# A fused two-block transformer kernel on one core: the second x chunk in two loads, and another order on each engine

## The chip, the cores and the metric

The kernel runs on one core of one Trainium2 chip. The metric is the time of one execution in device microseconds (us). The kernel before has a median of 393.72 us over three executions (392.11, 393.72 and 393.86). One further execution was profiled: 391.6 us, of which 389.9 us are the span between the first and the last instruction that the profile holds.

Five engines of the core take part: TensorE (PE, matrix products; PEld is its weight load), VectorE (DVE), ScalarE (ACT), GpSimd (POOL) and SyncE (SP), which here only issues DMA transfers. Each engine works through its own list in order. An instruction that waits for a semaphore holds up everything behind it in its list.

## The reference

The input is x of shape (1, 2048, 448) in bf16. Two kinds of block alternate, each with a residual connection: A (attention), B (gated), A, B, with the same weights both times.

```python
def _A_ref(x, wqkv, wo):
    B, S, D = x.shape
    H = 16; Dh = D // H
    W, dil = 8, 2
    qkv = (lambda x, *d: x.transpose(*d))((x @ wqkv).reshape(B, S, 3, H, Dh), 2, 0, 3, 1, 4)
    q, k, v = qkv[0], qkv[1], qkv[2]
    scale = Dh ** -0.5
    pos = jnp.arange(S)
    off = jnp.arange(W) * dil
    idx = pos[:, None] - off[None, :]
...
    logits = jnp.einsum("bhsd,bhswd->bhsw", q, kg) * scale
    logits = jnp.where(mask[None, None, :, :], logits, -1e9)
    attn = _softmax(logits, axis=-1)
    o = jnp.einsum("bhsw,bhswd->bhsd", attn, vg)
    return (lambda x, *d: x.transpose(*d))(o, 0, 2, 1, 3).reshape(B, S, D) @ wo

def _B_ref(x, w_gate, w_up, w_down):
    g = jnp.einsum("bsd,df->bsf", x, w_gate)
    u = jnp.einsum("bsd,df->bsf", x, w_up)
    h = g * u
    return jnp.einsum("bsf,fd->bsd", h, w_down)

x = x + _A_ref(_layernorm(x, axis=-1), A_wqkv, A_wo)
x = x + _B_ref(_layernorm(x, axis=-1), B_w_gate, B_w_up, B_w_down)
x = x + _A_ref(_layernorm(x, axis=-1), A_wqkv, A_wo)
x = x + _B_ref(_layernorm(x, axis=-1), B_w_gate, B_w_up, B_w_down)
```

## The kernel before

The 2048 tokens are 16 blocks of 128, and four blocks are a chunk. The input and output hold even tokens first, then odd ones, so that the dilated window of the attention becomes eight neighbours. The four layers run interleaved by chunks: `SEQ` is "A00 A01 B10 A02 B11 A03 B12 A20 ...", where A01 is layer 0 (attention), chunk 1, and B10 is layer 1 (gated), chunk 0.

**Of one attention chunk.** DVE computes the statistics of each block (L763 and L765), ACT the inverse deviation (L766, L768), and DVE writes the normalised block `xn_sb` (L784). In chunks 0 and 1 of layer 0 (`PE_T`) PE transposes it with an identity matrix (L794), and ACT or DVE copies the result to `xnTa` (L801). Elsewhere SP issues a DMA that transposes (L787). PE then computes K and Q in four units per chunk (L834, weights `WQK`), which ACT or DVE copies out of PSUM to `qk` (L895), and V (L834, weights `WV`; copied by L948). Scores (L981) of a group of queries occupy four PSUM banks. ACT takes the exponential (L993), DVE multiplies by the mask (L1002), and PE applies the result to V (L1020). DVE and ACT normalise (L1044 to L1070). PE multiplies with the output weights `wo_g` (L854 or L1106), and DVE adds to `x_sb` (L1114).

**Of one gated chunk.** The normalised block is written twice over (`xn_sb` of 896 columns) and transposed by DMA to `xnTb` (L787). PE computes gate and up together (L1144, weights `WGU`), ACT copies the gate (L1150), DVE multiplies (L1153) into `hT`, and PE computes the down product (L854, weights `WD`). The first product of L1144 waits for all 14 loads of `WGU` and for the four transposes of its chunk.

**PSUM** has eight banks, and most work takes them in pairs. A pair comes free when its reader on ACT or DVE is through.

**At the start** PE multiplies zeros (L683) until data arrive. SP and ACT issue the loads: x chunk 0 in four loads of one block, the V weights in four, the K and Q weights into `hT` in four (DVE and ACT reorder them into `WQK`, L692), and then x chunks 1, 2 and 3 in one load each. The load of chunk 1 waits for one of the V weight loads. The loads of `WGU` and `WD` wait until x block 7, the last of chunk 1, has landed.

**What sets the order.** Each unit of work gets a number as it is created (`Sched.add`). The table `ORDER` holds, for each engine, these numbers in the order in which the engine is to work. The scheduler then only assigns PSUM banks and semaphores. When a load is added, all numbers behind it shift by one.

Of the kernel before, what the change touches and what calls it, by code (L numbers as in the profile page):

```python
# [15 lines left out]
NCH = S // 512  # L16
# [53 lines left out]
    ],  # L70
    "act": [
# [12 lines left out]
    ],  # L84
    "dve": [
# [476 lines left out]
def build(nc, A_x, A_wqkv, A_wo, B_w_gate, B_w_up, B_w_down, out):  # L562
# [85 lines left out]
    for q in range(1, 4):  # L648
        load_x(q, (0, 1, 1), "sp", 4100.0, -50 + q, deps=[("wv", 3)] if q == 1 else [], svc=(1350.0 if q == 1 else 2600.0, 1200.0))
# [660 lines left out]
```

## Time and profile before

| what | us |
|---|---|
| median of three executions | 393.72 |
| the profiled execution | 391.6 |
| its span | 389.9 |
| PE busy within it | 379.3 |
| DVE busy | 263.8 |
| ACT busy | 184.0 |

All times below are of the profiled execution, counted from the start of its span. A row of the timeline gives start, duration, engine, line, operation, output and input, the number of instructions merged, and in brackets how long the engine sat idle before it and what ended that. The duration of a merged row runs to the end of its last instruction, and neighbouring rows overlap by about 0.1 us where the engine is pipelined. SPq marks the time in which SP issues a transfer; the transfer itself lands later.

### The profile page before, as it was taken

The page shows a single profiled execution, that of the slowest core. Times are in us where ns is not written, and L with a number is a line of the kernel's source. Part 1 is how long each engine was busy: PE and PEld are TensorE (multiplying, and loading weights), DVE is VectorE, ACT ScalarE, POOL GpSimd, SP SyncE. Part 2 cuts the span into 40 slices and gives each one's busy share as a digit, 9 for nine tenths or more (in the row PEclk, how much of TensorE's full clock was granted, in tenths as well). Part 3 has the DMA queues.
Part 4 walks back from the last instruction along what each step waited for, and adds up shares of the span by engine and source line. Part 5 has one row for each costly group of instructions (what it writes and reads, how often), then busy time and mean ns, then how long its engine had stood idle before and what let it go on. Part 6 is the DMA issues. An engine that isn't in the chain of part 4 may idle for free.

```text
span 389.9 us, 12779 instructions
## 1 busy us (share of the span) xinstructions
PE 379.3 (97%) x5694; PEld 201.2 (52%) x5694; DVE 263.8 (68%) x579; ACT 184.0 (47%) x302; POOL 6.0 (2%) x24
## 2 busy tenths in 40 slices
PE   7898999999999999999999999999999999999997
PEld 5454555555444555545444674445545555555554
DVE  6898879789897657355894278955478857733513
ACT  4996874772561336475143465332577303332310
POOL 6000000000000000000000000000000000000000
PEclk9999999999999999999999999999999999999999
DMA  7959675013142262000072000180001050310002
GB/s 218 266 104 159 98 128 134 3 26 74 25 72 59 30 87 57 11 6 5 5 108 43 14 6 5 24 126 5 12 2 45 19 96 13 79 41 2 13 0 96
DMA packets 53630, 22.59 MB, mean 58 GB/s; under 512 B 44288, under 2 KB 52648, under 8 KB 53576
## 3 DMA queue, kind: packets, MB, share of 16 engines
q1 hardware_dynamic: 52856, 21.15, 28.4%
q8 instruction: 45, 0.74, 0.8%
q10 hardware_dynamic: 720, 0.63, 0.5%
q14 instruction: 9, 0.07, 0.1%
HBM read 8.53 MB, written 1.84 MB: 27 GB/s over the span
## 4 chain that ended last, share of the span: by engine, by line
PE 90%; ACT 3%; DVE 3%; DMA 2%; issue 1%; SPq 1%
PE ps L1144 43%; PE ps L854 23%; PE ps L834 15%; PE ps L1106 3%; PE ps L1020 2%; PE ps L981 2%; PE ps L1165 1%; PE ps L683 1%; DMA xnTb<-xn_sb 1%; DMA qk<-qk 1%; DVE x_sb L1114 1%; ACT g_sb L1150 1%; ACT qk L895 1%; ACT E_sb L993 1%; SPq L619 1%
## 5 line engine op out<-in xcount | busy, mean ns | idle before, releaser
L1144 PE MATMUL ps<-xnTb,WGU 64*128 64x512 bf16 x1568 | 176.5, 376 | 0.8 <-DMA xnTb<-xn_sb 0.3
L1144 PEld LDWEIGHTS ps<-xnTb,WGU 64*128 64x128 bf16 x1568 | 81.1, 94 | 87.0 <-issue 4.2
L1150 ACT ACTIVATE g_sb<-ps 128x512 bf16<-128x512 f32 x112 | 64.9, 594 | 106.4 <-PE ps L1144 95.6
L1153 DVE TENSOR_TENSOR hT<-g_sb,ps 128x512 bf16<-128x512 bf16 x112 | 74.4, 681 | 51.2 <-ACT g_sb L1150 49.7
L854 PE MATMUL ps<-WD,hT 64*128 64x448 bf16 x840 | 85.7, 349 | 0.1
L854 PEld LDWEIGHTS ps<-WD,hT 64*128 64x128 bf16 x840 | 44.1, 94 | 34.6 <-DVE hT L1153 0.8
L1114 DVE TENSOR_TENSOR x_sb<-x_sb,ps 128x448 bf16<-128x448 bf16 x62 | 36.0, 614 | 30.0 <-PE ps L854 24.6
L834 PE MATMUL ps<-xnTa,WQK 64*128 64x512 bf16 (+1 forms) x448 | 47.2, 357 | 1.3 <-ACT E_sb L993 1.2
L993 ACT ACTIVATE E_sb<-ps 128x1024 bf16<-128x1024 f32 (+1 forms) x36 | 33.7, 980 | 17.9 <-PE ps L981 17.7
L763 DVE BATCH_NORM_STATS2 st<-x_sb 128x6 f32<-128x448 bf16 x64 | 38.2, 613 | 3.0 <-DMA x_sb<-in_A_x_dram 2.9
L784 DVE TENSOR_SCALAR xn_sb<-x_sb,mv,rstd 128x512 bf16<-128x512 bf16 (+1 forms) x64 | 34.8, 567 | 1.7 <-DMA xnTb<-xn_sb 1.0
L834 PEld LDWEIGHTS ps<-xnTa,WQK 64*128 64x128 bf16 x448 | 22.1, 94 | 23.0 <-ACT E_sb L993 2.7
L834 PE MATMUL ps<-WV,xnTa 64*128 64x448 bf16 (+1 forms) x252 | 28.1, 340 | 1.2 <-ACT lnv L766 0.8
L895 ACT ACTIVATE qk<-ps 128x1024 bf16<-128x1024 f32 (+1 forms) x24 | 22.8, 967 | 12.5 <-PE ps L834 12.4
L1070 DVE TENSOR_TENSOR oT<-ps,R_sb 128x448 bf16<-128x448 f32 (+2 forms) x38 | 21.1, 598 | 9.5 <-ACT R_sb L1050 9.5
L1002 DVE TENSOR_TENSOR E_sb<-E_sb,MK 128x1024 bf16<-128x1024 bf16 (+2 forms) x40 | 23.5, 604 | 3.3 <-ACT E_sb L993 3.2
L948 ACT ACTIVATE v_sb<-ps 128x896 bf16<-128x896 f32 (+1 forms) x16 | 13.7, 868 | 20.5 <-PE ps L834 20.4
L1049 ACT ACTIVATE R_sb<-R_sb 128x960 f32<-128x960 f32 (+1 forms) x18 | 17.3, 959 | 7.7 <-DVE R_sb L1047 7.5
L766 ACT ACTIVATE lnv<-mv,eps_sb 128x2 f32<-128x2 f32 (+1 forms) x34 | 9.2, 292 | 20.2 <-DVE mv L765 19.9
L834 PEld LDWEIGHTS ps<-WV,xnTa 64*128 64x128 bf16 x252 | 12.7, 94 | 11.2 <-issue 1.2
L1050 ACT ACTIVATE R_sb<-R_sb 128x960 f32<-128x960 f32 (+1 forms) x18 | 17.3, 959 | 0.4
L981 PEld LDWEIGHTS ps<-qk 28*64 28x64 bf16 x1088 | 10.1, 103 | 9.8 <-issue 4.8
(47 smaller groups left out, 172.6 us busy)
## 6 DMA issues: line engine op xcount, KB each, us to landing
out_dram<-x_sb SPq DMA_DIRECT2D x15, 112.0 KB, 1.8
WGU<-in_B_w_gate_dram SPq DMA_DIRECT2D x7, 224.0 KB, 5.1
WGU<-in_B_w_up_dram SPq DMA_DIRECT2D x7, 224.0 KB, 4.3
WD<-in_B_w_down_dram SPq DMA_DIRECT2D x14, 112.0 KB, 2.6
x_sb<-in_A_x_dram SPq DMA_DIRECT2D x3, 448.0 KB, 5.9
hT<-in_A_wqkv_dram SPq DMA_DIRECT2D x3, 224.0 KB, 5.0
qk<-qk SPq DMA_DIRECT2D x24, 28.0 KB
xnTb<-xn_sb SPq DMA_TRANSPOSE x32, 3.2
```

The source lines that it names most:

```text
L763: sc.add("dve", one(lambda E, B=B: E.bn_stats(st6[:, B, :], x_sb[:, B, :]), ("bn", li, B)), 525.0, deps=[("x", li - 1, B)] + ([("xn", li - ...
L784: sc.add("dve", one(lambda E, B=B, dst=dst, src=src: E.tensor_scalar(dst, src, mv[:, B, 0:1], rstd[:, B:B + 1], ALU.subtract, ALU.mult), ( ...
L834: ins.append((lambda E, w=w, c=c, lo=lo, st=st, sp_=sp_: E.matmul(u["out"](w), u["lhs"](w, c, lo, lo + 64), u["rhs"](w, c, lo, lo + 64), s ...
L854: ins.append((lambda E, w=w, c=c, lo=lo, st=st, sp_=sp_: E.matmul(outs(w), lhs(w, c, lo), rhs(w, c, lo), start=st, stop=sp_), keys[w] if s ...
L895: return E.activation(dst, src, ACT.Copy) if hasattr(E, "activation") else E.tensor_copy(dst, src)
L993: return E.activation(E_sb[:, slot, 2 * hp:2 * hp + 2, 0:w], ps[:, b0:b0 + 2, 0:w], ACT.Exp, scale=SCALE)
L1002: return E.tensor_tensor(e, e, m, ALU.mult)
L1070: return E.tensor_tensor(dst, src, rec, ALU.mult)
L1114: sc.add("dve", one(lambda E: E.tensor_tensor(x_sb[:, B, :], x_sb[:, B, :], ps[:, bk[w], 0:D], ALU.add), ("x", li, B)), dve_est(D), deps=[ ...
L1144: ins.append((lambda E, u=u, k=k, w=w: E.matmul(u["out"](w), WGU[64 * w:64 * w + 64, k, 128 * u["fc"]:128 * u["fc"] + 128], X[64 * w:64 * ...
L1150: sc.add("act", one(lambda E, gs=gs, bk=bk: E.activation(g_sb[:, gs, 0:n], ps[:, bk[0], 0:n], ACT.Copy), ("G", li, jp, fc)), act_est(n), d ...
L1153: sc.add("dve", one(lambda E, gs=gs, bk=bk, fc=fc: E.tensor_tensor(hT[:, fc, hs, h0:h1], g_sb[:, gs, 0:n], ps[:, bk[1], 0:n], ALU.mult), ( ...
```

## The change

The load of x chunk 1 (blocks 4 to 7, 448 KB) becomes two loads, blocks 4 and 5, then 6 and 7, each with a semaphore of its own. The first waits for the same V weight load as the whole chunk did. The loads of chunks 2 and 3 keep their form.

```diff
@@ build @@
-    sem_names += [f"d_x{i}0" for i in range(NCH)] + [f"d_x0{p}" for p in range(1, 4)] + ...
+    sem_names += [f"d_x{i}0" for i in range(NCH)] + [f"d_x0{p}" for p in range(1, 4)] + ["d_x11"] + ...
...
-    for q in range(1, 4):
-        load_x(q, (0, 1, 1), "sp", 4100.0, -50 + q, deps=[("wv", 3)] if q == 1 else [], svc=(1350.0 if q == 1 else 2600.0, 1200.0))
+    for h in range(2):
+        load_x(1, (h, h + 1, 2), "sp", 3450.0, -49.1 + 0.05 * h, deps=[("wv", 3)] if h == 0 else [], svc=(700.0, 1200.0))
+    for q in range(2, 4):
+        load_x(q, (0, 1, 1), "sp", 4100.0, -50 + q, svc=(2600.0, 1200.0))
```

The figures 3450, 700 and so on are the scheduler's estimates. With a written `ORDER` they set nothing in the program. The table `ORDER` itself is replaced for all five engines; its first lines for PE show how:

```diff
     "pe": [
-        38, 39, 40, 41, 42, 43, 44, 45, 46, 47, 48, 49, 50, 51, 52, 53, 54, 55, 56, 57, 58, 59, 60, 61, 62, 63, 142, 145, 64, 65, 148, 229, 66, 67, 230,
+        39, 40, 41, 42, 43, 44, 45, 46, 47, 48, 49, 50, 51, 52, 53, 54, 55, 56, 57, 58, 59, 60, 61, 62, 63, 64, 65, 66, 67, 68, 143, 69, 149, 146, 230,
...
```

No computation is added or removed. Line numbers behind the edit grow by three (L834 becomes L837, L1144 becomes L1147).

**ACT, in attention chunk 0 of layer 0, from the copy of the second V unit to the copies of the transposed blocks of chunk 1.** In these rows `qk` is the copy of a K and Q unit, and `xnTa` the copy of a block that PE transposed. Before:

```order
L948 ACTIVATE v_sb<-ps 128x32x28
L895 ACTIVATE qk<-ps 128x2x512
L766 ACTIVATE lnv<-mv,eps_sb 128x2
L692 ACTIVATE WQK<-hT 128x4x4x28
L768 ACTIVATE rstd<-lnv 128x2
L766 ACTIVATE lnv<-mv,eps_sb 128x2
L895 ACTIVATE qk<-ps 128x2x512
L768 ACTIVATE rstd<-lnv 128x2
L895 ACTIVATE qk<-ps 128x2x512
L801 ACTIVATE xnTa<-ps 128x4x128
L895 ACTIVATE qk<-ps 128x2x512
L801 ACTIVATE xnTa<-ps 128x4x128 x2
```

And now:

```order
L951 ACTIVATE v_sb<-ps 128x32x28
L695 ACTIVATE WQK<-hT 128x4x4x28 x2
L769 ACTIVATE lnv<-mv,eps_sb 128x2
L771 ACTIVATE rstd<-lnv 128x2
L898 ACTIVATE qk<-ps 128x2x512
L769 ACTIVATE lnv<-mv,eps_sb 128x2
L898 ACTIVATE qk<-ps 128x2x512
L771 ACTIVATE rstd<-lnv 128x2
L898 ACTIVATE qk<-ps 128x2x512
L804 ACTIVATE xnTa<-ps 128x4x128 x4
```

ACT copies three of the four K and Q units of chunk 0 and all four transposed blocks of chunk 1; before it was four units and three blocks.

**DVE, at the same place, up to the second pair of mask products.** `st` is the statistics of a block, `xn_sb` a normalised block, `E_sb<-E_sb,MK` the mask product. Before, from the first statistics of chunk 2, with four statistics and two normalisations of chunk 1 ahead:

```order
L763 BN_STATS st<-x_sb 128x6 x2
L784 TENSOR_SCALAR xn_sb<-x_sb,mv,rstd 128x512 x2
L763 BN_STATS st<-x_sb 128x6
L801 CAST xnTa<-ps 128x4x128
L763 BN_STATS st<-x_sb 128x6
L765 BN_AGGR mv<-st 128x2 x4
L763 BN_STATS st<-x_sb 128x6 x4
L1002 TENSOR_TENSOR E_sb<-E_sb,MK 128x2x288 x2
L784 TENSOR_SCALAR xn_sb<-x_sb,mv,rstd 128x512
L765 BN_AGGR mv<-st 128x2
L1002 TENSOR_TENSOR E_sb<-E_sb,MK 128x1024 x2
```

And now, from the last normalisation of chunk 1, with three statistics of chunk 2 already ahead of it:

```order
L787 TENSOR_SCALAR xn_sb<-x_sb,mv,rstd 128x512
L768 BN_AGGR mv<-st 128x2 x2
L898 CAST qk<-ps 128x2x512
L766 BN_STATS st<-x_sb 128x6 x2
L768 BN_AGGR mv<-st 128x2
L766 BN_STATS st<-x_sb 128x6 x2
L1005 TENSOR_TENSOR E_sb<-E_sb,MK 128x2x288 x2
L766 BN_STATS st<-x_sb 128x6
L1005 TENSOR_TENSOR E_sb<-E_sb,MK 128x1024
L787 TENSOR_SCALAR xn_sb<-x_sb,mv,rstd 128x512
L1005 TENSOR_TENSOR E_sb<-E_sb,MK 128x1024
```

DVE now copies a K and Q unit in place of a transposed block, and one set of statistics and one normalisation stand among the mask products.

**SP, from the last transposes of attention chunk 3 to the first loads of the down weights.** `qk<-qk` are the small moves that spread a quarter of Q over the partitions, `xnTb<-xn_sb` the transposes of gated chunk 0. Before:

```order
L787 DMA_TRANSPOSE xnTa<-xn_sb 128x4x128
L619 DMA qk<-qk 28x1x512 x2
L619 DMA WGU<-in_B_w_up_dram 64x1792
L619 DMA qk<-qk 28x1x512 x2
L787 DMA_TRANSPOSE xnTb<-xn_sb 128x7x128 x4
L619 DMA WD<-in_B_w_down_dram 128x448
```

And now:

```order
L790 DMA_TRANSPOSE xnTa<-xn_sb 128x4x128 x4
L620 DMA qk<-qk 28x1x512 x3
L790 DMA_TRANSPOSE xnTb<-xn_sb 128x7x128
L620 DMA qk<-qk 28x1x512
L790 DMA_TRANSPOSE xnTb<-xn_sb 128x7x128
L620 DMA WGU<-in_B_w_gate_dram 64x1792
L790 DMA_TRANSPOSE xnTb<-xn_sb 128x7x128 x2
L620 DMA WD<-in_B_w_down_dram 128x448 x6
```

The last move of Q and the last load of `WGU` now stand behind transposes of gated chunk 0.

More of the change, by code (lines that the diff above doesn't have):

```diff
@@ L55 @@
     "pe": [
[14 rows of a table removed]
[14 rows of a table added]
     ],
     "act": [
[12 rows of a table removed]
[12 rows of a table added]
     ],
     "dve": [
[19 rows of a table removed]
[20 rows of a table added]
     ],
     "pool": [
-        23, 22, 24, 32, 19, 25, 26, 27, 18, 33, 28, 21, 20, 29, 30, 31, 34, 35, 36, 37,
+        25, 26, 33, 24, 29, 30, 34, 22, 20, 27, 31, 19, 23, 35, 21, 28, 36, 32, 37, 38,
     ],
     "sp": [
[7 rows of a table removed]
[7 rows of a table added]
     ],
@@ L603, in build @@
     sem_names = ["pe", "act", "dve", "pool"]
-    sem_names += [f"d_x{i}0" for i in range(NCH)] + [f"d_x0{p}" for p in range(1, 4)] + [f"d_{n}{c}" for n in ("stg", "wv") for c in range(4)] + ["d_wo", "d_wg", "d_wu", "d_wd0", "d_wd1", "d_out", "d_out2"]
+    sem_names += [f"d_x{i}0" for i in range(NCH)] + [f"d_x0{p}" for p in range(1, 4)] + ["d_x11"] + [f"d_{n}{c}" for n in ("stg", "wv") for c in range(4)] + ["d_wo", "d_wg", "d_wu", "d_wd0", "d_wd1", "d_out", "d_out2"]
     sem_names += [f"d_t1_{j}b" for j in range(NCH) if any(f"B{li}{j}a" in SEQ for li in (1, 3))]
```

103 rows, old and new, of the table ORDER are left out of this document.

## The prediction

> **What bounds the kernel now.** I read the page first: which engine is full, and what the chain that ended last consists of.
>
> ```profile
> span 389.9 us, 12779 instructions
> PE 379.3 (97%) x5694; PEld 201.2 (52%) x5694; DVE 263.8 (68%) x579; ACT 184.0 (47%) x302; POOL 6.0 (2%) x24
> PE 90%; ACT 3%; DVE 3%; DMA 2%; issue 1%; SPq 1%
> ```
>
> PE is busy for 379.3 of 389.9 us, and 90% of the chain is PE. The change removes no PE work, so a gain can only come out of the 10.6 us in which PE is idle, and a loss can only come as new idle time there. The windows tell where those 10.6 us lie.
>
> ```profile
> core 0: us, PE busy (x) PEld busy (x) DVE busy (x) ACT busy (x) POOL busy (x), PEclk, DMA share, GB/s
> 0.00:60.00 60.00, 54.30 (x1106) 29.31 (x1108) 49.90 (x136) 45.38 (x74) 6.04 (x24) 1.00 0.79 164
> 60.00:380.00 320.00, 317.52 (x4528) 167.04 (x4526) 210.28 (x437) 138.60 (x229) 0.00 (x0) 1.00 0.20 37
> 380.00:389.90 9.90, 7.50 (x64) 4.84 (x60) 3.61 (x7) 0.00 (x0) 0.00 (x0) 1.00 0.29 94
> ```
>
> The first 60 us hold 5.7 us of idle PE, the last 10 us hold 2.4 (the last results on their way out), and the 320 us between hold only 2.5. The granted clock is 1.00 throughout. So the first 60 us decide, and I followed them in the timeline.
>
> ```profile
> 7.07 0.94 SPq L619 DMA_DIRECT2D x_sb<-in_A_x_dram  x2
> DMA to landing us min/median/max: 4.2/5.0/5.9
> 8.51 2.11 DVE L692 COPY WQK<-hT 128x112 bf16<-128x112 bf16 x9
> 11.26 1.15 DVE L763 BATCH_NORM_STATS2 st<-x_sb 128x6 f32<-128x448 bf16 x2 [0.65 <-DMA x_sb<-in_A_x_dram]
> 14.77 1.15 DVE L763 BATCH_NORM_STATS2 st<-x_sb 128x6 f32<-128x448 bf16 x2
> 17.11 1.02 ACT L895 ACTIVATE qk<-ps 128x1024 bf16<-128x1024 f32 x1
> 18.04 1.08 ACT L801 ACTIVATE xnTa<-ps 128x512 bf16<-128x512 f32 x2
> 18.19 0.34 PE L981 MATMUL ps<-qk 28*64 28x72 bf16 x32 [0.79 <-ACT qk L895]
> 18.35 0.36 DVE L765 BATCH_NORM_AGGREGATE mv<-st 128x2 f32<-128x6 f32 x4
> 18.63 2.17 DVE L763 BATCH_NORM_STATS2 st<-x_sb 128x6 f32<-128x448 bf16 x4
> 19.17 0.71 PE L981 MATMUL ps<-qk 28*64 28x64 bf16 x64 [0.64 <-ACT xnTa L801]
> 19.81 3.20 PE L834 MATMUL ps<-xnTa,WQK 64*128 64x512 bf16 x28
> 20.72 0.81 DVE L1002 TENSOR_TENSOR E_sb<-E_sb,MK 128x576 bf16<-128x576 bf16 x2
> 21.45 0.41 DVE L784 TENSOR_SCALAR xn_sb<-x_sb,mv,rstd 128x512 bf16<-128x512 bf16 x1
> 21.86 1.48 DVE L1002 TENSOR_TENSOR E_sb<-E_sb,MK 128x1024 bf16<-128x1024 bf16 x2
> 27.74 1.21 DVE L895 CAST qk<-ps 128x1024 bf16<-128x1024 f32 x1
> ```
>
> The second row is from the view of `x_sb` for the loads of the first row: chunk 1, issued at 7.07, lands 4.2 us later, and chunk 2, issued about 0.45 us behind it, lands after 5.9, at 13.4. DVE is through with the weight copies at 10.62 and waits 0.65 for chunk 1. PE, however, has K and Q work until 17.1; it stands still later, before the two score groups at 18.19 and 19.17, and both times for ACT.
>
> **Part 1, the split load.** 448 KB separate the landings at 11.26 and 13.4, that is 2.1 us, so half a chunk takes about 1.05 us and blocks 4 and 5 land at 10.2. Bounds: 10.2, and 11.26 if the two halves run mixed and end together. I take 10.2, since chunks 1 and 2 landed one behind the other. Then DVE starts its statistics at 10.62, 0.64 us earlier (bounds 0 and 0.64). Blocks 6 and 7 are wanted 1.3 us later and lie there from 11.3 on. The additional issue, 0.47 us by the first row, stands between work that waits for nothing on SP; chunk 2, which it moves back, is wanted at 14.1 (14.77 less 0.64) and lands at 13.4 to 13.9.
>
> The row says that a half needs 1.05 us. The Trainium skill, "DMA: Bandwidth & Descriptors", section "Anatomy of one DMA", puts a fixed 2 us on each transfer and moves the rest at 436 GB/s, and its section "Rules for kernel authors" advises large transfers; by its rate (an estimate from that page) the first half would be only 0.5 us ahead, at 10.7, DVE 0.08 us later than I take it, and the sum for the head -0.1 in place of -0.2. The landings here go at the slower pace, and the trace decides.
>
> **Part 2, ACT and DVE share the copies anew.** DVE takes over one copy of a K and Q unit (1.21 us) and gives one of a transposed block to ACT. On DVE, 14.1 is followed by three statistics (0.54 each, from 2.17 for four), two normalisations (0.35 net of overlap) and three small aggregations (0.1), then the copy: 14.1 + 1.6 + 0.7 + 0.3 + 1.2 = 17.9. The first scores wait for that and start at 17.9 in place of 18.19. ACT, one copy lighter (0.92 net of overlap) and one block heavier (0.5), ends its four blocks at about 18.3, so the second scores start at 18.4 in place of 19.17. K and Q of chunk 1 then wait for banks, until the first exponential is through: at about 19.25, 0.55 us before 19.81.
>
> But the next step waits for DVE. In its new list stand, behind the copy at 17.9, five statistics (2.7), an aggregation (0.1), the first mask products (0.73), one large one (0.65), a normalisation (0.36), and only then the mask product on which the second half of L1020 depends: it starts at 22.4 and ends at 23.05. Before, it ended at 23.34 by the rows (21.86 + 1.48). Of the 0.55 us PE thus keeps 0.25. Bounds: 0.55 kept if DVE is quicker, 0.4 lost if the halves land together (DVE 0.64 later than reckoned). I take **-0.2**.
>
> **Part 3, what SP issues between 41 and 57 us.**
>
> ```profile
> 42.77 1.52 SPq L619 DMA_DIRECT2D qk<-qk  x2
> 42.79 0.93 PE L834 MATMUL ps<-WV,xnTa 64*128 64x448 bf16 x8
> 44.91 1.34 SPq L619 DMA_DIRECT2D qk<-qk  x2
> 45.85 1.14 DVE x_sb L1114 x2
> 46.99 1.06 DVE st L763 x2
> 46.30 6.55 SPq L787 DMA_TRANSPOSE xnTb<-xn_sb  x4
> 48.19 0.72 DVE xn_sb L784 x2
> 49.53 1.21 DVE oT L1070 x2
> 50.30 0.71 PE L981 MATMUL ps<-qk 28*64 28x64 bf16 x64
> 50.74 0.66 DVE xn_sb L784
> DMA to landing us min/median/max: 3.0/3.9/4.5
> 51.55 4.01 DMA xnTb<-xn_sb
> 55.80 1.69 PE L1144 MATMUL ps<-xnTb,WGU 64*128 64x512 bf16 x14 [0.31 <-DMA xnTb<-xn_sb]
> 163.72 3.51 DMA qk<-qk
> DMA to landing us min/median/max: 3.3/3.3/3.3
> ```
>
> These are the timeline and the chain of waits, with the landing times of the four `xnTb` transposes and, in the last row, of the `WGU` load issued at 44.33. The first gate product starts at 55.80 after 0.31 us of idle PE, when the last transpose lands (issued at 51.55, 4.0 us under way).
>
> The last move of Q is now issued behind a transpose, which takes 1.3 us to issue (6.55 for four, waits included): at about 46.2 to 47 in place of 45.6. With the 3.5 us that such a move took in the chain at 163.72 it lands at 49.7 to 50.5, against the scores at 50.30: 0 to 0.2 us; I take **0**, the slack covers it. The last load of `WGU` comes behind the second transpose, at about 48.3, and lands at 51.6 by the last row, hidden by PE's work until 55.5.
>
> The last transpose: DVE's additions at 45.85 come one V unit later (8 matmuls, 0.75 us net of overlap), since PE now does that unit first. On the other hand two normalisations that came between them and the last one are done earlier. From 46.6: additions and statistics 2.3, the pass of L1070 1.2, the last two normalisations 1.35: 51.5, and SP, which issues two transposes then, gets to the last at 52.2 in place of 51.55. With 3.0 to 4.0 us it lands at 55.2 to 56.2, less the 0.2 that PE is ahead. PE gets there at 55.3. Against 55.80 that is from -0.4 to +0.3; **+0.1**, near the upper end because the transposes share the queue with the load of `WGU`.
>
> **Part 4, the rest.** The lists of the 320 us that follow exchange neighbours of one kind; the same groups of scores still wait behind the same number of products. I count **0**, with bounds of 1.2 either way, half of the 2.5 us of idle PE. At the end the order of the last down products changes, and one half block becomes the last; **0**.
>
> The sum is -0.2 + 0.1, about -0.1 us: a span of 389.8, an execution of 391.5. The profiled execution is 2.1 us below the median of the three, so against that the same sum gives 393.6.
>
> **Rivals.** (A) *The stalls of the head go for good.* If the DVE list keeps up, PE keeps 0.55 us at 19.81; the 0.31 at 55.80 goes too, and two further waits shrink:
>
> ```profile
> 32.37 0.82 PE L834 MATMUL ps<-xnTa,WQK 64*128 64x512 bf16 x6 [1.15 <-ACT E_sb L993]
> 292.53 0.71 PE L981 MATMUL ps<-qk 28*64 28x64 bf16 x64 [0.77 <-ACT g_sb L1150]
> ```
>
> All of it: 0.55 + 0.31 + 1.15 + 0.77 = 2.8; I put it at 2.4, to 391.3. For it speaks that four short waits are within reach of a better order; against it, that the same instructions stand ahead of these two places as before.
>
> (B) *The first gate product waits for SP.* One mechanism: SP's list is in order, and the transpose that now stands before the last move of Q waits for DVE. If DVE is late there, Q, the second transpose, the last load of `WGU` and the two last transposes all move. With the last transpose one transpose's issue (1.3 us) and one load's issue (0.6, the way from the load at 44.33 to the next row at 44.91) later than I reckon, and the longest way of the four to landing, it lands at 52.2 + 1.3 + 0.6 + 4.5 = 58.6, 2.8 later than 55.80; less the 0.2 of the head, 396.3. It decides from 57.8 on (2 us). For it: the last landing ends PE's wait there already, without slack. Against: the two normalisations that SP waits for are moved forward.
>
> (C) *The halves do not land apart.* Then DVE starts at 11.26 as before but carries the longer list, +0.4 in place of -0.2: 394.2. For it: both halves are issued within 0.47 us of each other and share the same 16 engines. Against: chunks 1 and 2 did the same and landed 2.1 us apart.
>
> **How the numbers follow.** A measurement of this kernel can tell about 0.5% from no change, 2 us. Forecast: 0.36, 393.6, its own range 391.9 to 395.6; of it 0.05 falls below and 0.06 above the 0.5%. A 0.24, all of it faster. B 0.28, nearly all slower (0.26). C 0.12, of it 0.02 slower. Together: faster 0.29, within 0.37, slower 0.34. The range runs from 390.2, a little below A, to 397.4, above B; about 1 in 10 lies outside at each side.
>
> **What would show it.** Statistics of x chunk 1 at 10.6 without a wait for a DMA bear out part 1; a wait until 11.2 is C. Scores at 17.9 and 18.4 and K and Q at 19.25 bear out the first half of part 2, and the second half of L1020 at 23.0 its second half. The first gate product within 0.4 us of 55.7 bears out part 3; at 57.8 or later it is B. Idle PE of 2 to 3 us between 60 and 380 us bears out part 4. The prediction is wrong if a new wait of more than 2 us stands before a product anywhere, or if the idle time of the first 60 us falls below 4 us.

## The result, and the profile after

| kernel | median us | executions | ratio to before, 95% interval |
|---|---|---|---|
| before, beside the changed kernel | 392.50 | 20 (391.36 to 394.52) | |
| changed | 394.34 | 20 (393.23 to 395.65) | 1.0041 [1.0026, 1.0056] |

The change makes the kernel slower by 0.41%, some 1.6 us (the medians differ by 1.8). That is inside the 0.5% within which the prediction put its forecast, but it is not the "no change" of its sum (-0.1 us): with twenty executions of each, the interval excludes that. That its 393.6 lies near the measured 394.34 is luck: the number was reckoned on the median of three early executions, 393.72; on 392.50 the same sum gives 392.4. The profiled execution of the changed kernel has a span of 392.3 us against 389.9. These 2.4 us are more than the change costs on the whole, since the profiled execution before (391.6) was 0.9 us faster than its median. Two executions of the experiments below, one of the split alone and one with the loads at the old places, took 492 us at a granted clock of 0.75 to 0.76 and are left out of the ratios.

The first two lines of the page after, and its line on the queue that carries instructions:

```profile
span 392.3 us, 12781 instructions
PE 380.7 (97%) x5694; PEld 198.3 (51%) x5694; DVE 266.7 (68%) x582; ACT 180.7 (46%) x299; POOL 5.8 (1%) x24
q8 instruction: 45, 0.74, 0.9%
```

The windows after, with the columns as before:

```profile
0.00:60.00 60.00, 53.00 (x1084) 28.57 (x1086) 49.33 (x134) 41.43 (x70) 5.84 (x24) 1.00 0.78 159
60.00:380.00 320.00, 317.96 (x4528) 163.33 (x4524) 213.72 (x442) 139.25 (x230) 0.00 (x0) 1.00 0.21 38
380.00:392.30 12.30, 9.79 (x89) 6.37 (x84) 3.61 (x7) 0.00 (x0) 0.00 (x0) 1.00 0.23 76
```

Between 60 and 380 us PE now idles 2.0 us in place of 2.5, and at the end 2.5 in place of 2.4. The loss lies in the first 60 us, where PE idles 7.0 us in place of 5.7 and 22 products fewer get done than before (1084 against 1106). The timeline of PE there, after:

```profile
18.66 1.05 PE L984 MATMUL ps<-qk 28*64 28x72 bf16 x96 [0.92 <-DVE qk L898]
19.87 3.19 PE L837 MATMUL ps<-xnTa,WQK 64*128 64x512 bf16 x28 [0.16 <-ACT E_sb L996]
23.00 0.24 PE L1023 MATMUL ps<-E_sb,v_sb 64*32 64x72 bf16 x10
24.46 0.98 PE L1023 MATMUL ps<-E_sb,v_sb 64*32 64x72 bf16 x86 [1.22 <-issue]
25.37 3.20 PE L837 MATMUL ps<-xnTa,WQK 64*128 64x512 bf16 x28
32.82 0.82 PE L837 MATMUL ps<-xnTa,WQK 64*128 64x512 bf16 x6 [0.44 <-DMA xnTa<-xn_sb]
37.56 2.15 PE L837 MATMUL ps<-xnTa,WQK 64*128 64x512 bf16 x19
41.34 2.33 PE L837 MATMUL ps<-xnTa,WQK 64*128 64x512 bf16 x23 [1.64 <-issue]
43.31 0.93 PE L837 MATMUL ps<-WV,xnTa 64*128 64x448 bf16 x6
53.44 0.70 PE L984 MATMUL ps<-qk 28*64 28x64 bf16 x64 [0.21 <-DMA qk<-qk]
58.19 1.67 PE L1147 MATMUL ps<-xnTb,WGU 64*128 64x512 bf16 x14
```

And the rows of the same work before that the prediction does not show:

```profile
22.93 1.21 PE L1020 MATMUL ps<-E_sb,v_sb 64*32 64x72 bf16 x96
24.08 3.20 PE L834 MATMUL ps<-xnTa,WQK 64*128 64x512 bf16 x28
37.00 4.68 PE L834 MATMUL ps<-xnTa,WQK 64*128 64x512 bf16 x42
41.32 0.93 PE L834 MATMUL ps<-WV,xnTa 64*128 64x448 bf16 x6
```

Set side by side, the lateness builds up at two places. K and Q of chunk 1 start 0.06 us later (19.87 against 19.81). Then a run of 96 small products of L1023, which had gone through in one piece, stops after 10, for 1.22 us, and the next K and Q start 1.29 later (25.37 against 24.08). Most of that is absorbed at 32.82, where PE before had waited 1.15 us (for an exponential, by the profile) and now waits 0.44 for a transpose: 0.45 late there, 0.56 at 37.56. The second stop, 1.64 us, falls in the middle of the 42 products of a K and Q unit, and V follows 1.99 later (43.31 against 41.32). The first gate product is 2.39 later (58.19 against 55.80), and so is the end (2.4).

Both stops are of a peculiar kind. "issue" says that PE waited for nothing that the profile shows, and the chain of waits of the changed kernel passes through both:

```profile
23.07 0.17 PE ps L1023 x10
23.23 1.22 issue
...
37.62 2.08 PE ps L837 x19
39.70 1.64 issue
```

They begin in the midst of the instructions of one unit of work. What moved ahead of them is on SP. After, from 30 us on:

```profile
29.93 2.46 SPq L620 DMA_DIRECT2D WGU<-in_B_w_gate_dram  x2
32.44 0.60 SPq L620 DMA_DIRECT2D WGU<-in_B_w_up_dram  x1
33.08 1.24 SPq L620 DMA_DIRECT2D WGU<-in_B_w_gate_dram  x2
34.35 0.60 SPq L620 DMA_DIRECT2D WGU<-in_B_w_up_dram  x1
34.99 6.03 SPq L790 DMA_TRANSPOSE xnTa<-xn_sb  x4
```

Before it was four loads of `WGU` (30.66 to 33.2) ahead of the transposes, with a fifth behind the third of them. The last of the six now lands at 40.96; before, the last of the four landed at 37.17.

**The theory.** The page's queue q8 carries 45 packets of 16 KB, and PE has 11513 instructions in the trace, 256 for each packet: PE's own program, which is fetched while it runs. (The Trainium skill, "Runtime: NRT & Kernel Launch", section "Instruction fetch mechanics", says the same: refills in blocks of 16 KiB, 256 instructions, the next block while the current one runs. It calls the cost of crossing a block "mostly hidden"; here it was not.) The page counts these packets as a share of the same 16 DMA engines as the loads. The theory, F: where many loads are under way, the fetch comes late, and PE stops at the end of its block. Its rivals: D, the new lists of PE, ACT and DVE cost the time; S, the split itself does; B, the prediction's own rival, SP's order from 45 us on; T, the two places wait for something that belongs to their operation.

The trace holds the fetch packets one by one. PE's instructions are counted from 0 at the start of the span, products and weight loads together:

```
            block fetched   PE reaches the     fetch packet      PE stops before   PE goes on
                            block before it                      instruction
before      705 to 960      18.21 (no. 449)    20.76 to 22.03    -                 -
changed     705 to 960      18.68              21.53 to 22.83    705               24.46
before      1473 to 1728    35.83 (no. 1217)   36.99 to 38.10    1473 (0.11 us)    39.36
changed     1473 to 1728    36.29              38.65 to 39.97    1473              41.34
```

In each stop PE resumes 1.3 to 1.6 us behind the end of the packet, and the two stops are 768 instructions apart, 3 x 256. From no. 1217 to 1473 PE has only 3.0 us of work (36.29 to 39.33), because the block holds most of 128 short products of scores and of L1023. A packet takes 1.1 to 1.3 us and 1.3 to 1.6 more pass until PE goes on, so this block has nearly no room for a late fetch.

### The profile page after: what moved, and what is told of

Same layout as the page of the kernel before. It is cut to its first block, busy times and chain, and to the rows that moved or that the text cites. A ratio compares the mean times of both kernels' runs of the same rounds, so it can differ in the third digit from the quotient of the medians.

```text
span 392.3 us, 12781 instructions
## 1 busy us (share of the span) xinstructions
PE 380.7 (97%) x5694; PEld 198.3 (51%) x5694; DVE 266.7 (68%) x582; ACT 180.7 (46%) x299; POOL 5.8 (1%) x24
## 4 chain that ended last, share of the span: by engine, by line
PE 91%; ACT 2%; DVE 2%; DMA 2%; issue 1%; SPq 0%
PE ps L1147 43%; PE ps L857 23%; PE ps L837 15%; PE ps L1109 3%; PE ps L984 3%; PE ps L1023 3%; PE ps L686 2%; PE ps L1168 1%; DMA xnTa<-xn_sb 1%; DMA qk<-qk 1%; ACT R_sb L1053 1%; ACT E_sb L996 0%; ACT R_sb L1052 0%; ACT g_sb L1153 0%; DVE R_sb L1050 0%
## 5 line engine op out<-in xcount | busy, mean ns | idle before, releaser
L1147 PE MATMUL ps<-xnTb,WGU 64*128 64x512 bf16 x1568 | 176.2, 376 | 0.3
L1147 PEld LDWEIGHTS ps<-xnTb,WGU 64*128 64x128 bf16 x1568 | 80.0, 94 | 88.4 <-issue 4.9
L857 PEld LDWEIGHTS ps<-WD,hT 64*128 64x128 bf16 x840 | 42.7, 94 | 35.7 <-DVE hT L1156 0.5
L837 PE MATMUL ps<-xnTa,WQK 64*128 64x512 bf16 (+1 forms) x448 | 47.1, 356 | 2.3 <-issue 1.6
L787 DVE TENSOR_SCALAR xn_sb<-x_sb,mv,rstd 128x896 bf16<-128x896 bf16 (+1 forms) x64 | 35.0, 566 | 5.7 <-ACT rstd L771 3.2
L837 PEld LDWEIGHTS ps<-xnTa,WQK 64*128 64x128 bf16 x448 | 21.8, 94 | 24.0 <-issue 2.1
L837 PE MATMUL ps<-WV,xnTa 64*128 64x448 bf16 (+1 forms) x252 | 28.1, 339 | 0.9 <-ACT xnTa L804 0.4
L898 ACT ACTIVATE qk<-ps 128x1024 bf16<-128x1024 f32 x21 | 21.0, 1020 | 16.7 <-PE ps L837 16.7
L837 PEld LDWEIGHTS ps<-WV,xnTa 64*128 64x128 bf16 x252 | 11.8, 94 | 12.1 <-PE ps L837 1.6
L898 DVE CAST qk<-ps 128x512 bf16<-128x512 f32 (+1 forms) x11 | 10.1, 929 | 11.0 <-PE ps L837 11.0
L1053 ACT ACTIVATE R_sb<-R_sb 128x960 f32<-128x960 f32 (+1 forms) x18 | 17.2, 957 | 0.3
L951 ACT ACTIVATE v_sb<-ps 128x896 bf16<-128x896 f32 (+1 forms) x14 | 11.9, 860 | 9.0 <-PE ps L837 8.9
```

The lines of the kernel that those rows point to most:

```text
L787: sc.add("dve", one(lambda E, B=B, dst=dst, src=src: E.tensor_scalar(dst, src, mv[:, B, 0:1], rstd[:, B:B + 1], ALU.subtract, ALU.mult), ( ...
L837: ins.append((lambda E, w=w, c=c, lo=lo, st=st, sp_=sp_: E.matmul(u["out"](w), u["lhs"](w, c, lo, lo + 64), u["rhs"](w, c, lo, lo + 64), s ...
L857: ins.append((lambda E, w=w, c=c, lo=lo, st=st, sp_=sp_: E.matmul(outs(w), lhs(w, c, lo), rhs(w, c, lo), start=st, stop=sp_), keys[w] if s ...
L898: return E.activation(dst, src, ACT.Copy) if hasattr(E, "activation") else E.tensor_copy(dst, src)
L1053: sc.add("act", one(lambda E: E.activation(flat, flat, ACT.Exp, scale=-1.0), ("R", li, g)), act_est(4 * n * nr, False), deps=[("Rl", li, g ...
L1147: ins.append((lambda E, u=u, k=k, w=w: E.matmul(u["out"](w), WGU[64 * w:64 * w + 64, k, 128 * u["fc"]:128 * u["fc"] + 128], X[64 * w:64 * ...
```

## The experiments

The numbers in SP's list: 98 to 111 are the loads of `WGU` (gate even, up odd), 83 to 86 those of `wo_g`, 191 to 197 and 211 to 217 (odd) the transposes of chunks 2 and 3 of `xnTa`, 404 to 407 the Q moves, 331 to 337 (odd) the transposes of `xnTb`. Each run was compared with the kernel before on the same chip; the ratios are to it. The first four rows, the next three, the next two and the last two were taken on four different chips, so ratios and not times compare across these sets.

| kernel | us | ratio, 95% interval |
|---|---|---|
| split alone | 392.51 | 0.9995 [0.9977, 1.0012] |
| changed, loads at the old places | 394.19 | 1.0036 [1.0019, 1.0053] |
| old lists, loads at the new places | 394.13 | 1.0036 [1.0021, 1.0051] |
| changed, three loads later | 392.98 | 1.0002 [0.9986, 1.0018] |
| changed, five loads later | 392.03 | 0.9987 [0.9973, 1.0000] |
| changed, 128 PE instructions more | 394.46 | 1.0064 [1.0025, 1.0103] |
| changed, three loads later, Q first | 391.92 | 0.9991 [0.9972, 1.0010] |
| changed, five loads later, Q first | 392.19 | 0.9987 [0.9967, 1.0006] |
| old lists, split, loads spread | 391.17 | 0.9965 [0.9944, 0.9986] |
| the same once more | 390.87 | 0.9969 [0.9953, 0.9985] |
| before, loads spread, no split | 391.45 | 0.9981 [0.9964, 0.9998] |

**The split alone.** All lists of before, renumbered, and in SP's:

```diff
-    ... 12, 14, 85, ...
+    ... 12, 13, 14, 85, ...
```

> The kernel before with nothing but the split: the second half of x chunk 1 is issued right behind the first, all lists of all engines are otherwise those of before. Theory F (PE runs out of fetched instructions at about its 690th and its 1473rd instruction, because the fetch of its next 16 KB of program waits in the DMA engines behind loads of WGU): the loads of WGU stand where they stood, so the two stalls that nothing in the profile ends stay at 0.1 to 0.6 us each, and the time is within 0.2% of before, 392.0 to 393.0 when before is at 392.5. Theory D (the new lists of PE, ACT and DVE cost the time): the same. Theory S (the split itself, one more issue on SP ahead of everything else, costs it): 0.3 to 0.5% slower, with the loss complete by 20 us.

The ratio is 0.9995: S falls, and the split brings nothing by itself either. The first scores start at 18.11 against 18.19. One of the two stops is there already, 0.64 us before instruction 705 (fetch 21.09 to 22.34), a little above the 0.6 expected at most. The other is not: its fetch starts at 36.43, when PE has entered the block ahead at 36.30.

**The loads at the new places, under the old lists.** The lists of before with the split; on SP the transposes of each chunk in before's sequence, but the loads standing where the changed kernel has them, and the last Q move and the last load of `WGU` behind transposes of `xnTb`, as there:

```diff
-    ..., 84, 108, 98, 106, 83, 99, 100, 103, 86, 191, 101, 195, 197, 107, 193, 111, 102, 109, 110, 215, 211, 217, 104, 213, 404, 407, 105, 405, 406, 331, 333, 337, ...
+    ..., 109, 83, 108, 102, 84, 86, 99, 101, 107, 191, 195, 111, 197, 193, 106, 104, 105, 98, 110, 103, 215, 211, 217, 213, 404, 407, 405, 331, 406, 333, 100, 337, ...
```

> The mirror image: the split and the lists of PE, ACT and DVE of before, but the loads of WGU and wo_g on SP at the places of the changed kernel (six loads of WGU in a row behind the transpose near 29 us). F: the two stalls without a releaser appear here too, together over 1.5 us, and the time is 0.2 to 0.5% above before. D: as before, within 0.2%. B: 0.2 to 0.5% slower too, but by a wait of the scores near 50 us or of the first gate product for a DMA, without the stalls.

PE's timeline of this kernel:

```profile
41.50 2.32 PE L837 MATMUL ps<-xnTa,WQK 64*128 64x512 bf16 x23 [1.84 <-issue]
59.10 1.26 PE L1147 MATMUL ps<-xnTb,WGU 64*128 64x512 bf16 x10 [1.41 <-DMA xnTb<-xn_sb]
```

The whole loss is there with the old lists (1.0036). The second stop came as F says, before instruction 1473 again; the first did not show (the granted clock was 0.83 between 20 and 30 us of this execution, see the last section, which left that fetch more time). A second price came with it that F had not named and B had: the first gate product waits 1.41 us for a transpose that stands behind the last Q move and the last load of `WGU`. The run does not part the two.

**The loads at the old places, under the new lists.** The mirror image: the changed kernel's lists and its sequence of transposes, the loads where before has them.

```diff
-    ..., 109, 83, 108, 102, 84, 86, 99, 101, 107, 193, 195, 111, 197, 191, 106, 104, 105, 98, 110, 103, 211, 213, 215, 217, 404, 407, 405, 333, 406, 331, 100, ...
+    ..., 84, 108, 98, 106, 83, 99, 100, 103, 86, 193, 101, 195, 197, 107, 191, 111, 102, 109, 110, 211, 213, 215, 104, 217, 404, 407, 105, 405, 406, 333, 331, ...
```

> The changed kernel's lists of PE, ACT and DVE, and its own order of transposes, but the loads of WGU and wo_g on SP at the places of before, up to the last transpose of the first half of xnTb (the last Q move again ahead of the first of these transposes). F: the stalls without a releaser near 23 and 40 us fall from 1.22 and 1.64 to 0.6 or less each, the first gate product starts 2 us earlier than in the changed kernel (56.2), time about 392.3, within 0.2% of before. D: the time stays 0.3 to 0.5% above before. B (SP's order from 45 us on makes the loss): the stalls stay, the scores at 53.4 come about 2 us earlier, and the time falls by 1 to 2 us for that reason.

```profile
25.46 0.89 PE L1023 MATMUL ps<-E_sb,v_sb 64*32 64x72 bf16 x86 [0.23 <-issue]
34.74 0.82 PE L837 MATMUL ps<-xnTa,WQK 64*128 64x512 bf16 x6 [1.40 <-DMA xnTa<-xn_sb]
58.90 1.47 PE L1147 MATMUL ps<-xnTb,WGU 64*128 64x512 bf16 x12 [0.73 <-DMA xnTb<-xn_sb]
```

This is F's miss. The stops went, from 1.22 to 0.23 and from 1.64 to none, and the time stayed at 1.0036. (The clock was 0.83 between 20 and 30 us here too, so the first stop may owe its shrinking to that; the second lies behind it.) The old places put loads between the transposes of chunk 2, and under the new lists PE then waits 1.40 us for the last of those (0.44 in the changed kernel), and 0.73 at the first gate product (none there). So the loss is not tied to the fetch alone. As these rows read, loads delay whatever stands behind them, transposes too, and which late transfer PE meets depends on the lists. That is read from an execution with a clock dip; the five at a clock of 1.000 have a mean of 393.68, against 392.40 for before, so the loss is there without the dip, but no trace shows where it lies in them.

**Three loads later.** One edit to the changed kernel:

```diff
-    106, 104, 105, 98, 110, 103, 211, 213, 215, 217, 404,
+    106, 104, 105, 211, 213, 215, 217, 98, 110, 103, 404,
```

> The changed kernel with one edit: of the six loads of WGU that SP issues in a row from 30 us on, the last three go behind the four transposes that follow. F: the second stall (1.64 us, near 40) falls to 0.6 or less, the first (1.22, near 23) stays between 0.8 and 1.5; the first gate product starts about 1.3 us earlier, at 56.9; time 0.3% below the changed kernel, about 393. D: nothing changes, 394.3. B: the three loads now come nearer to the moves of Q, which can only make the last of these later: 394.3 or more.

```profile
24.88 0.89 PE L1023 MATMUL ps<-E_sb,v_sb 64*32 64x72 bf16 x86 [1.54 <-issue]
33.45 0.82 PE L837 MATMUL ps<-xnTa,WQK 64*128 64x512 bf16 x6 [0.65 <-DMA xnTa<-xn_sb]
```

1.0002: the loss is gone, by moving three loads and nothing else. The second stop has vanished (fetch at 36.99, when PE enters the block at 36.92, in place of 2.4 us behind it), the first is still there, 1.54 us before instruction 705. D, which kept the lists, expected no change and falls as the whole of the story.

**Five loads later.** Two of the six loads issued from 10.9 to 16.5 us go the same way:

```diff
-    86, 99, 101, 107, 193, ..., 104, 105, 98, 110, 103, 211, 213, 215, 217, 404,
+    86, 99, 193, ..., 104, 105, 211, 213, 215, 217, 101, 107, 98, 110, 103, 404,
```

> The kernel of the three late loads, with two more loads of WGU (of the six that are issued from 10.9 to 16.5 us) behind the last transpose of xnTa, five there in all. F: with two loads fewer in the DMA engines the fetch that PE waits for near 23 us starts 1.5 to 2 us earlier, and the first stall (1.54 us with three late loads) falls to 0.5 or less; the second stays away. Time about 1.2 us below that kernel, 391.6 when before is at 392.6, unless the five loads, which now land between 42 and 48 us, delay the Q moves or the first transposes of xnTb; those would show as a wait of the scores near 52 or of the first gate product for a DMA. D: the time of the kernel with three late loads, 392.9.

```profile
23.22 0.68 PE L1023 MATMUL ps<-E_sb,v_sb 64*32 64x64 bf16 x64 [0.18 <-ACT qk L898]
32.18 0.82 PE L837 MATMUL ps<-xnTa,WQK 64*128 64x512 bf16 x6 [1.34 <-DMA xnTa<-xn_sb]
58.07 1.69 PE L1147 MATMUL ps<-xnTb,WGU 64*128 64x512 bf16 x14 [0.91 <-DMA xnTb<-xn_sb]
```

The first stop has gone as well: the fetch starts at 19.48, 1.1 us behind the point where PE enters the block (18.38). Time 0.9987, some 0.6 us below the kernel with three late loads by the ratios, where 1.2 was expected, and with intervals that overlap even that is not shown. PE, earlier now, waits 1.34 us for the last transpose of chunk 2, and 0.91 at the first gate product for a transpose behind the five late loads (in an execution whose clock was 0.89 between 30 and 45 us).

**128 PE instructions more.** The warm-up products cut in two, nothing else (the zeros that they multiply are used by nobody):

```diff
-        ins = [(... warm[lo:lo + 64, :] ...) for h in range(2)]
+        ins = [(... warm[lo:lo + 64, c:c + 128] ...) for c in (0, 128) for h in range(2)]
```

> The changed kernel, its lists untouched, but each of the 64 warm-up products of 256 columns ahead of the first data is cut into two of 128: the same work, and 128 PE instructions more (64 products and their weight loads) ahead of everything. F: the stalls stand at fixed places of PE's program, so they come at the same number of PE instructions as before, about the 705th and the 1473rd, and so 128 instructions earlier among the work: the 1.64 us near 40 us between K and Q units of chunk 2 are gone there (under 0.4), the 1.22 us in L1023 near 23 us too, and a new stall without a releaser can stand in K and Q of chunk 1 at 20 to 21 us. Time 392.5 to 393.8. Rival T (these two places wait for something that belongs to their operation, which the profile does not name): both stalls stay where they are, before the same products, and the time is 394.3.

```profile
25.20 0.28 PE L1023 MATMUL ps<-E_sb,v_sb 64*32 64x64 bf16 x22 [1.12 <-issue]
38.26 0.52 PE L1023 MATMUL ps<-E_sb,v_sb 64*32 64x64 bf16 x45 [1.56 <-issue]
```

The stops are before instructions 961 and 1473. The second has the very number that it had before, and so falls 128 instructions earlier in the work, out of K and Q and into the run of L1023 ahead of it. The first is a full block behind its old place in the count (705 + 256): the boundary of 705 now lies where the fetch was in time (14.70 to 16.09), and the next one has come into the short products of L1023. T falls. The expected place of the first was wrong (20 to 21 us was named), and so was the time (1.0064, not below the changed kernel): the stops moved, and together they cost 2.7 us in place of 2.9. Three smaller ones came further on:

```profile
78.18 0.36 PE L837 MATMUL ps<-WV,xnTa 64*128 64x448 bf16 x1 [0.25 <-issue]
182.71 1.50 PE L857 MATMUL ps<-WD,hT 64*128 64x448 bf16 x14 [0.26 <-issue]
236.76 1.12 PE L857 MATMUL ps<-WD,hT 64*128 64x448 bf16 x10 [0.51 <-issue]
```

They stand before instructions 3009, 6337 and 7873, all multiples of 256 behind 1473, and PE goes on 1.3 to 1.4 us after the packet's end in each. The changed kernel has no stop there, so they explain up to 1.0 us of the time that was not expected.

**Q first.** The kernel with three late loads, with SP's order from 41 us on changed back in part:

```diff
-    217, 98, 110, 103, 404, 407, 405, 333, 406, 331, 100, 335,
+    217, 100, 98, 110, 103, 404, 407, 405, 406, 333, 331, 335,
```

> The kernel of the three late loads with SP's order from 41 us on put back in part: the last load of WGU goes ahead of the Q moves, and the last Q move ahead of the first transpose of xnTb. B (part 3 of the prediction, SP's order there, costs time): the scores near 52 us and the first gate product start 0.5 to 1 us earlier, time 0.2% below the kernel with three late loads. F: no more than the 0.42 us that PE idles at the first gate product can go, time within 0.1% of it.

0.9991 against 1.0002, with intervals that overlap: B's 0.2% is neither shown nor excluded. The first gate product came at 56.05 in place of 57.33, of which 0.45 is a shorter first stop (1.09 against 1.54).

**Both remedies.** The kernel with five late loads, and behind them:

```diff
-    404, 407, 405, 333, 406, 331, 100, 335,
+    404, 407, 405, 406, 100, 333, 331, 335,
```

> The kernel of the five late loads with the last Q move and the last load of WGU ahead of the first transpose of xnTb: the two remedies together. F: neither stall without a releaser above 0.4 us before 45 us, scores near 52 us without a wait for a DMA; the first gate product at 55 to 56.5 us; time 391.0 to 391.8, that is 0.2 to 0.4% below before. If the transposes of xnTb are slowed by the five loads all the same, a wait of about 0.9 us for them stays at the first gate product, and the time is 392, as with the five late loads alone.

0.9987, the case that the expectation put second: no stop without a releaser is left (with a clock of 0.83 between 20 and 30 us in the execution shown by its profile), and the first gate product waits 0.81 us for a transpose. The remedies do not add.

**The old lists, with the loads spread.** The split alone, with six loads moved on SP (one less ahead of the transposes of chunk 2, one less between them, one less ahead of those of chunk 3, and five behind these):

```diff
-    99, 100, 103, 86, 191, 101, 195, 197, 107, 193, 111, 102, 109, 110, 215, 211, 217, 104, 213, 404, 407, 105, 405,
+    99, 100, 86, 191, 101, 195, 197, 193, 107, 111, 102, 215, 211, 217, 213, 104, 109, 110, 105, 103, 404, 407, 405,
```

> The kernel before with the split, lists of PE, ACT and DVE as before, and on SP one load of WGU fewer ahead of the transposes at 22 us, one fewer between them, and five behind the last transpose of xnTa. F: the stall of 0.64 us at 23.7 that the split alone showed falls to 0.3 or less, and the wait of 1.28 us for a transpose at 32.8 to the 1.15 us by which an exponential ends it anyway; time 0.1 to 0.3% below before. D (lists decide, loads don't): as before, within 0.1%. If the five late loads come in the way of the Q moves, the scores at 50.3 or the first gate product wait for a DMA, and the time is before's or more.

> The kernel with the old lists, the split and the spread loads once more, beside the one without the split: 0.2 to 0.5% below before again if its first result holds; with F equal to the kernel without the split within 0.15%.

Of the second execution that was profiled:

```profile
24.41 0.98 PE L1023 MATMUL ps<-E_sb,v_sb 64*32 64x72 bf16 x85 [0.37 <-issue]
32.51 0.82 PE L837 MATMUL ps<-xnTa,WQK 64*128 64x512 bf16 x6 [0.18 <-DMA xnTa<-xn_sb]
56.06 1.69 PE L1147 MATMUL ps<-xnTb,WGU 64*128 64x512 bf16 x14 [0.69 <-DMA xnTb<-xn_sb]
```

0.9965 and 0.9969, twice below before with intervals clear of 1: the fastest kernel of the study, 0.7% below the changed one by the two ratios (0.9969 / 1.0041). The stop before instruction 705 is 0.37 (0.3 or less was expected). The wait at 32 us, 1.15 before and 1.28 with the split alone, has shrunk to 0.18. Before's row put it down to an exponential, but here K and Q of chunk 2 start at 32.51 while the exponential behind the same scores runs from 32.40 to 33.42. So, as far as these rows show, they had depended on when the last transpose landed: at 32.23 before, where PE went on at 32.37.

**The same moves without the split.** Before's own table with the six loads moved:

> The kernel before, x chunk 1 in one load as it was, with nothing but the six loads of WGU moved on SP as in the kernel with the old lists and spread loads. F (the loads ahead of the fetches and transposes make the difference, the split none): 0.2 to 0.4% below before, within 0.15% of that kernel. S' (the split is what makes the spread loads pay, since half a chunk lands earlier): within 0.1% of before.

0.9981 [0.9964, 0.9998]: the spread loads pay without the split. The split's own share, 0.9969 against 0.9981, is within the intervals and stays open.

## Why the prediction was wrong

**What bounds the kernel** was read rightly: the first 60 us decided, and the idle time of the rest stayed at 2.0 us, within the 2 to 3 named.

**Part 1 held.** DVE and the halves of chunk 1, after:

```profile
10.37 1.14 DVE L766 BATCH_NORM_STATS2 st<-x_sb 128x6 f32<-128x448 bf16 x2
16.03 0.41 DVE L787 TENSOR_SCALAR xn_sb<-x_sb,mv,rstd 128x512 bf16<-128x512 bf16 x1 [0.41 <-ACT rstd L771]
17.29 1.23 DVE L898 CAST qk<-ps 128x1024 bf16<-128x1024 f32 x1 [0.30 <-PE ps L837]
```

The halves landed at 9.53 and 10.86 (issued at 6.75 and 7.18), chunk 2 at 13.38, and the statistics start without a wait for a DMA. The halves came 1.3 us apart, not 1.05, and not the 0.5 of the estimate from the Trainium skill. (The section that the prediction names there, "Anatomy of one DMA" of "DMA: Bandwidth & Descriptors", is by its heading on transfers issued by GpSimd; these were issued by SP.) Rival C falls. But the split alone was worth nothing that could be measured.

**Part 2 was mis-sized.** "17.9 + ..." added up DVE's work ahead of its copy of a K and Q unit. The row shows that the copy waited for PE instead, and this is the unit it waited for:

```profile
16.18 1.04 PE L837 MATMUL ps<-xnTa,WQK 64*128 64x512 bf16 x8
```

PE is through with it at 17.2 (16.18 + 1.04), a little later than before (16.01 + 1.04). With 1.23 us for the copy, no list that leaves it to DVE could have had the scores before 18.4; they came at 18.66, and K and Q of chunk 1 at 19.87 in place of the predicted 19.25. The whole 0.55 us was never to be had: the term of -0.2 measured +0.06 at this place. What was to follow from it, L1023's second half at 23.0, was overtaken by the first stop.

**Part 3 looked at the right queue in the wrong stretch.** It followed SP from 41 to 57 us. The change also moved the loads of `WGU` between 11 and 41 us, and for these the sum had no term. The one load that it priced, the last, it priced by when it lands and when PE wants it ("hidden by PE's work until 55.5"), not by what stands behind it in the DMA engines. That is the step that failed. What the term should have held is in the runs: two stops of PE, 1.22 and 1.64 us, less the 0.84 that the old wait at 32 us took up (1.29 late ahead of it, 0.45 behind), some 2.0 us by 43 us; moving three loads took the loss back. Of the rest up to 58 us (0.4), 0.21 is a wait of the scores for the last Q move, which landed at 53.3 (3.64 us under way from 49.66, by the chain) instead of the 49.7 to 50.5 predicted. The first gate product passed B's mark of 57.8, but not by B's mechanism: it does not wait there for anything.

**Part 4 held** for the 320 us behind, which gained 0.4 us in place of 0, and for the end (0.1).

**The list of what would show it** had the sentence that came closest, "a new wait of more than 2 us before a product". Two of 1.2 and 1.6 came, and no engine or transfer of the kernel's own was at their end. B, A and C named no such wait either: the prediction had no rival for the fetch of PE's program.

What stays open: how the old and the new lists of PE, ACT and DVE compare with loads that hinder neither. The best kernel with the new lists has 0.9987, with the old 0.9965; the loads do not stand alike in the two, and the executions differ in their share of clock dips (see the last section).

## What to carry to other kernels

A transfer that nobody waits for was not free here: with several large loads in a row, ask what is queued behind them in the DMA engines, transposes and small moves as well as the instruction fetch of a busy engine. Suspect a late fetch where a stop ends in "issue" in the middle of one unit's instructions, at a place that is a multiple of 256 instructions from the next such stop. Here the two long ones came behind blocks that were short in time, with runs of small matrix products. Weights that are wanted late are best issued where neither such a block nor a transpose on the critical path is due; here moving three to six load issues was worth 0.2 to 0.4%.

## What was not expected of the hardware

PE had its program only about one block ahead, and ran out of it. In every stop of more than 0.2 us in the first 60 us that nothing in the profile ended, the instruction at which PE stopped was 705, 961 or 1473 by the count of the trace (differences 256 and 512), and PE resumed 1.3 to 1.6 us after the fetch packet had ended: 24.46 after 22.83, 41.34 after 39.97, in the kernel with more instructions 25.20 after 23.81 and 38.26 after 36.94. In all thirteen profiled executions, with 45 packets each, PE never starts on a block sooner than 1.2 us after the end of its packet. The packets behind these stops took 1.1 to 1.5 us; what varied was when a packet started, from about the moment at which PE entered the block ahead (three late loads, 36.99 against 36.92) to 3.5 us behind it (35.59 against 32.10, with 128 instructions more).

In some executions the granted clock fell in the head. The window of the kernel with the loads at the old places, where the clock is the third figure from the end:

```profile
20.00:30.00 10.00, 9.60 (x184) 4.22 (x173) 8.31 (x31) 7.81 (x16) 0.00 (x0) 0.83 0.66 116
```

A clock of 0.83 over 10 us is 3.4 us at half speed. (The Trainium skill, "TensorE: Matmul & The Clock Gate", Part 1, gives a free-running window of 3413 ns after which an idle PE is put to half its clock; the length agrees, but PE was not idle for a whole window here.) PE had idled 0.94 us before the scores just ahead, and from 16.6 to 20.0 us it was busy for 2.05 of 3.4 us. Of the executions of before beside the first four experiments, 25 of 35 show a mean clock of 0.996 or less, and of the changed kernel 4 of 20. At a clock of 1.000 alone, before has a mean of 392.40 (10 executions) and the changed kernel 394.20 (16), though not measured side by side; the dip is not what made it slower. It does bear on the small differences among the experiments. Each kernel at 1.000 against before at 1.000 beside it: three late loads 392.54 against 392.40, five late loads 391.94 against 392.01, both remedies 392.08 against 391.86. So the 0.9987 of these last two comes from dips that before has more of, and the late loads bring the changed kernel back to before, not below it. The spread loads stay ahead at 1.000 too: 390.71 against 391.86, 390.68 against 391.96 once more, and 391.00 against 391.96 without the split.
